# Shifting the ranks of a list scheduler's operations by a table, for two attention layers in one kernel

## The chip, the cores and the metric

The kernel runs on one core of a Trainium2 chip. The metric is device microseconds of one execution, as the median of several runs. The core has five engines that work side by side: PE (matmuls), DVE (VectorE), ACT (ScalarE), POOL (GpSimd) and SP (SyncE), which here issues every transfer. Each engine takes its instructions strictly in the order in which the program lists them, and engines wait for each other through semaphores. So the order written down for each engine is part of the program, and this change touches that order and nothing else.

## The reference: two attention layers, side by side

Both halves work on 2048 tokens of width 1024 with 32 heads of 32, and the result is their outputs next to each other.

```python
def _A_ref(x, wq, wk, wv, wo, beta):          # four segments of 512 tokens
    ...
    for s in range(N):
        qs, ks, vs = q[:, :, s], k[:, :, s], v[:, :, s]
        logits = jnp.einsum("bhqd,bhkd->bhqk", qs, ks) * scale + mask
        p = _softmax(logits, axis=-1)
        a_dot = jnp.einsum("bhqk,bhkd->bhqd", p, vs)
        pq = phi(qs)
        num = jnp.einsum("bhld,bhde->bhle", pq, M)
        den = jnp.einsum("bhld,bhd->bhl", pq, z)[..., None] + 1e-6
        outs.append(g * (num / den) + (1.0 - g) * a_dot)
        pk = phi(ks)
        M = M + jnp.einsum("bhld,bhle->bhde", pk, vs)
        z = z + jnp.einsum("bhld->bhd", pk)
    ...
    return o @ wo

def _B_ref(x, wqkv, w_phi, wo):               # linear attention
    ...
    pq = jnp.einsum("bhsd,hdf->bhsf", q, w_phi)
    pk = jnp.einsum("bhsd,hdf->bhsf", k, w_phi)
    phi_q = concatenate([_softmax(pq), _softmax(-pq)])
    phi_k = concatenate([_softmax(pk), _softmax(-pk)])
    kv = jnp.einsum("bhsf,bhsd->bhfd", phi_k, v)
    z  = jnp.einsum("bhsf->bhf", phi_k)
    o = einsum(phi_q, kv) / (einsum(phi_q, z)[..., None] + 1e-6)
    return o @ wo
```

## The kernel before

**Number formats.** Matmuls run in float16. An operand is scaled and split into a high and a low half, and a product is three matmuls (high by high, high by low, low by high: `product`, L370). The splits keep ACT (the high half), DVE or POOL (the low half) busy. The large projections of the second layer and the last projection of the first are Strassen products: seven instead of eight block products (`strassen`, L584 for its matmuls, and L1636 at the end).

**Stages.** First come 32 *units* of the first layer, one segment and four heads each (`produce`, `values`, `attend`). `produce` projects queries and keys (L370) and sends them by DMA into a stacked tile. `attend` forms scores twice: once to find row maxima (L846, with the masked maximum on DVE at L852), which go back as extra rows (L867, L872), and once for the exponentials (L947, ACT L951 and L953, DVE L954 for the low half, POOL L960 for the triangular mask). Then p times v (L983, summed by DVE at L987), the memory terms (L899 to L926) and the transposed result (L1015). Between them stand the folding of the weights of the second layer (`fold`, L1088, with the size at L1094), the splitting of its value weights (`weights_v`) and of its tokens, in pairs of tiles (`prepare`, L1134 and behind).

Then the pool of tiles is swapped for another, and eight pairs of token tiles go through keys and values of the second layer: a Strassen product (L584), the double softmax (`expo`: maxima and minima L1238, differences L1240 and L1242, exponentials L1245, sums L1248), the product with the inverse sums on POOL (L1354), a split (L1386, L1389) and the sums over tokens (L1396). Tile pairs 3, 4 and 5 are prepared only here, on the POOL lines L1153 and L1164. Next, the key sums are spread and split (L1419, L1440, L1443, L1445), and sixteen query tiles follow in the same way (L1550 to L1588), with an output projection each (`project`, L370 again). Eight Strassen products at L1636 end the kernel.

**What sets the order.** The code does not issue instructions where it describes them. It records each operation with its engine, a cost in microseconds, what it reads and writes, and a rank `prio` (`Graph.op`, L115). When all 16810 are recorded, `Graph.run` (L160) goes through them as a list scheduler: it keeps a clock for each engine, takes the engine that could start something first, and there, of the operations that could start by that time, the one with the lowest rank (ties go to the one that was recorded first). It counts latencies between engines, transfers on their queue, the port that DVE and POOL can't use at once, and the eight PSUM banks, which it hands out as it goes; for PE it prefers operations whose inputs are there with 0.4 us to spare. Only then is the instruction issued. In a unit u of the first layer the ranks are 2u for the projections, 2u + 0.9 for the values and 2u + 1 for attention; the keys of the second layer start at 100 and count 2 for a pair; the queries start at 118 and count 1 for a tile (a Strassen product has the rank of its tile less 1.2, a projection that of its tile and 1.1); the end has 135 and more.

Of the kernel before, what the change touches and what calls it, by code (L numbers as in the profile page):

```python
# [53 lines left out]
WPLAN = ((None, 0, 0), (None, 2, 1), (None, 3, 5), ((1, 0, "subtract"), 0, 3), ((3, 1, "subtract"), 1, 4),  # L54
         ((3, 0, "subtract"), 3, 2), ((2, 3, "subtract"), 2, 6))
EUP = 2.0 ** 15


def view(t, off, ap):
# [3 lines left out]
class Buf:  # L63
    def __init__(self, make, prev):
        self.make, self.prev, self.t = make, prev, None
        self.ops, self.writer, self.readers = [], {}, {}
        self.kind = None
# [11 lines left out]
class Graph:  # L79
# [10 lines left out]

    def __init__(self, pools):
        self.ops, self.tags, self.pools, self.opened, self.lines = [], {}, pools, {}, {}

    def buf(self, pool, shape, dtype, tag, bufs=1):
        q = self.tags.setdefault(tag, [])
        b = Buf(lambda: self.pools[pool].tile(shape, dtype, name=tag, tag=tag, bufs=bufs),
                (q[-bufs] if len(q) >= bufs else None, q[-1] if q else None, self.opened.get(pool)))
        q.append(b)
        return b
# [13 lines left out]
        return b  # L113

    def op(self, eng, dur, fn, r=(), w=(), prio=0, lat=0.0, short=False, port=False, need=(), kb=256):  # L115
        o = Op()
        o.short, o.port = short, port or eng == "POOL"
        o.eng, o.dur, o.fn, o.prio, o.lat, o.kb = eng, dur, fn, (prio, len(self.ops)), lat, kb
        o.banks = []
        ends, starts = set(), set()  # L120
        for b in need:
            if b.prev[0] is not None:
                ends.update(b.prev[0].ops)
        for write, accs in ((0, r), (1, w)):
            for acc in accs:
                b, key = acc if isinstance(acc, tuple) else (acc, None)
                old, last, opened = b.prev
                if old is not None:
                    ends.update(old.ops)
                if not b.ops and last is not None:  # L130
                    starts.add(last.ops[0])
                if opened is not None:
                    starts.add(opened)
                for k in (list(b.writer) if key is None else [key, None]):
                    if k in b.writer:
                        ends.add(b.writer[k])
                if write:
                    for k in (list(b.readers) if key is None else [key, None]):
                        ends.update(b.readers.pop(k, ()))
                    if key is None:  # L140
                        b.writer.clear()
                    b.writer[key] = o
                else:
                    b.readers.setdefault(key, []).append(o)
                b.ops.append(o)
                if b.kind is not None and b not in o.banks:
                    o.banks.append(b)
                    b.left += 1
        ends.discard(o)
        o.deps = [(d, 0) for d in ends] + [(d, 1) for d in starts - ends if d is not o]  # L150
        self.ops.append(o)
        return o
# [99 lines left out]
SP, PE, ACT, DVE, POOL = "SP", "PE", "ACT", "DVE", "POOL"  # L252
# [3 lines left out]
def tile_kernel(ctx: ExitStack, tc: tile.TileContext, ax, aw, awv, awo, beta, bx, bwqk, bwv, bphi, bwo, out):  # L256
# [70 lines left out]
    for t in vfb:  # L327
# [6 lines left out]
    gate1 = const.tile([128, H], F32, name="gate1")  # L334
    gates = G.fixed(gate)
    op(SP, 0.6, lambda: nc.sync.dma_start(gate, bass.AP(tensor=beta.tensor, offset=beta.offset, ap=[[0, 128], [1, H]])),
       w=[gates], prio=0.2, lat=2.0, kb=16)
    op(ACT, 0.2, lambda: nc.scalar.activation(gate, gate, AF.Exp, bias=0.0, scale=-1.0), w=[gates], prio=0.2)
    op(DVE, 0.2, lambda: nc.vector.tensor_scalar(gate, gate, 1.0, None, op0=OP.add), w=[gates], prio=0.2)
    op(DVE, 0.3, lambda: nc.vector.reciprocal(gate, gate), w=[gates], prio=0.2)  # L340
    op(DVE, 0.2, lambda: nc.vector.tensor_scalar(gate1, gate, -1.0, 1.0, op0=OP.mult, op1=OP.add), w=[gates], prio=0.2)
# [883 lines left out]
    def expo(ps, prio, sk, up=None):  # L1225
        port = ps not in psums

        def x3():
            return ps().rearrange("p (h d) -> p h d", d=32)

        def rep(v):
            return v[:, :, None].to_broadcast([128, 16, 32])

        mx = G.buf("b", [128, 2, 16], F32, "mx", 2)
        e = G.buf("b", [128, 16, 2, 32], F32, "e", 5)
        r = G.buf("b", [128, 16, 2], F32, "r", 5)
        for i, o in ((0, OP.max), (1, OP.min)):
            op(DVE, 0.6, lambda i=i, o=o: nc.vector.tensor_reduce(mx()[:, i, :], x3(), axis=AX.X, op=o),  # L1238
               r=[ps], w=[(mx, i)], prio=prio)
        op(DVE, 0.6, lambda: nc.vector.tensor_tensor(e()[:, :, 0, :], x3(), rep(mx()[:, 0, :]), op=OP.subtract),  # L1240
           r=[ps, (mx, 0)], w=[(e, 0)], prio=prio, port=port)
        op(DVE, 0.6, lambda: nc.vector.tensor_tensor(e()[:, :, 1, :], rep(mx()[:, 1, :]), x3(), op=OP.subtract),  # L1242
           r=[ps, (mx, 1)], w=[(e, 1)], prio=prio, port=port)
        for i in range(4):
            op(ACT, 0.41, lambda i=i: nc.scalar.activation(  # L1245
                e()[:, 4 * i:4 * i + 4], e()[:, 4 * i:4 * i + 4], AF.Exp, bias=0.0, scale=sk()[:, i:i + 1]),
               r=[e, sk], w=[(e, ("x", i))], prio=prio)
        op(DVE, 1.13, lambda: nc.vector.tensor_reduce(r(), e(), axis=AX.X, op=OP.add), r=[e], w=[r], prio=prio)  # L1248
        if up is not None:
            op(POOL, 0.15, lambda: nc.gpsimd.tensor_scalar(r(), r(), 1.0 / up, None, op0=OP.mult), r=[r], w=[r], prio=prio)  # L1250
        op(DVE, 0.27, lambda: nc.vector.reciprocal(r(), r()), r=[r], w=[r], prio=prio)
        return e, r

    def bc32(r):
        return r()[:, :, :, None].to_broadcast([128, 16, 2, 32])
# [86 lines left out]
    for at_, p in enumerate(SEQ):  # L1342
# [9 lines left out]
        def kout(i, hb, ps, es=es, sk=sk, P=P):  # L1352
            e, r = expo(ps, P, sk, EUP)
            op(POOL, 1.95, lambda: nc.gpsimd.tensor_tensor(e(), e(), bc32(r), op=OP.mult), r=[e, r], w=[e], prio=P)  # L1354
            es[i, hb] = e
# [60 lines left out]
    for q in range(4):  # L1416
        ps = bank("misc", [128, 512])
        for i in range(4):
# [3 lines left out]
        op(ACT, 0.5, lambda q=q, ps=ps: nc.scalar.activation(  # L1422
            zb()[:, 4 * q:4 * q + 4, :].rearrange("p a b -> p (a b)"), ps(), AF.Copy, scale=1.0 / EUP), r=[ps], w=[(zb, q)], prio=P)
    op(DVE, 0.1, lambda: nc.vector.tensor_reduce(big[:, 1:2], big[:, 1:6], axis=AX.X, op=OP.max),
# [283 lines left out]
```

## Time and profile before

| what | value |
|---|---|
| median of 3 runs | 1734.23 us (1733.72 to 1735.37) |
| the profiled execution | 1733.96 us |
| its span, first to last instruction | 1732.3 us |
| PE busy | 1697.2 us, 98% |
| DVE busy | 1384.0 us, 80% |
| ACT busy | 1157.8 us, 67% |
| POOL busy | 939.5 us, 54% |
| transfers | 273.62 MB |
| instructions | 39104 |

The span is what the trace shows from its first instruction to its last; the execution is 1.7 us longer. A row of a group names the line, the engine, the operation, the tile written and the tile read, their shapes, the number, then the busy time, the mean of one in ns, and the idle time ahead of them with what ended it. A row of the waits reads: who waited, for whom, microseconds in total, how often, the longest. A row of a stretch gives its start and end, its length, the busy time of PE, weight loads, DVE, ACT and POOL with the number of instructions, the granted share of PE's clock, the busy share of the DMA engines, and GB/s. A row of the timeline gives the start, the time taken, and then the operation.

### The profile page before, as it was taken

The page shows a single profiled execution, that of the slowest core. Times are in us where ns is not written, and L with a number is a line of the kernel's source. Part 1 is how long each engine was busy: PE and PEld are TensorE (multiplying, and loading weights), DVE is VectorE, ACT ScalarE, POOL GpSimd, SP SyncE. Part 2 cuts the span into 40 slices and gives each one's busy share as a digit, 9 for nine tenths or more (in the row PEclk, how much of TensorE's full clock was granted, in tenths as well). Part 3 has the DMA queues.
Part 4 walks back from the last instruction along what each step waited for, and adds up shares of the span by engine and source line. Part 5 has one row for each costly group of instructions (what it writes and reads, how often), then busy time and mean ns, then how long its engine had stood idle before and what let it go on. Part 6 is the DMA issues. An engine that isn't in the chain of part 4 may idle for free.

```text
span 1732.3 us, 39104 instructions
## 1 busy us (share of the span) xinstructions
PE 1697.2 (98%) x14664; PEld 1030.3 (59%) x14664; DVE 1384.0 (80%) x3269; ACT 1157.8 (67%) x2131; POOL 939.5 (54%) x1184
## 2 busy tenths in 40 slices
PE   8999999999999999999999999999999999999999
PEld 6667666767776676776754444444545555554444
DVE  6889899999997787889874988877978877786541
ACT  8788889888888798677772676765545544444331
POOL 3346477754478866656651777645737675440000
PEclk9999999999999999999999999999999999999999
DMA  6556455775666664743467474567413332234311
GB/s 210 160 166 185 151 169 174 223 209 169 224 181 185 188 165 122 227 162 106 136 179 262 131 240 130 180 211 251 161 44 118 103 111 85 63 139 146 122 66 63
DMA packets 194141, 273.62 MB, mean 158 GB/s; under 512 B 72224, under 2 KB 125216, under 8 KB 187424
## 3 DMA queue, kind: packets, MB, share of 16 engines
q1 hardware_dynamic: 193952, 271.13, 49.5%
q8 instruction: 115, 1.88, 0.4%
q14 instruction: 74, 0.61, 0.1%
HBM read 160.12 MB, written 85.00 MB: 142 GB/s over the span
## 4 chain that ended last, share of the span: by engine, by line
PE 40%; DVE 11%; ACT 2%; POOL 1%; issue 1%; POOLq 0%; ACTq 0%; DVEq 0%
PE proj L584 14%; PE misc L370 7%; PE proj L1636 5%; PE s L1636 2%; PE proj L370 2%; PE s L584 2%; DVE mx L1238 2%; PE misc L1636 1%; DVE r L1248 1%; PE pv L1582 1%; PE misc L584 1%; PE s L1569 1%; DVE e L1240 1%; DVE dn L1553 1%; DVE e L1242 1%; DVE pt L1389 1%
## 5 line engine op out<-in xcount | busy, mean ns | idle before, releaser
L370 PE MATMUL proj<-S,S 128*128 128x128 f16 (+1 forms) x3072 | 507.1, 300 | 4.3 <-DVE S L405 1.9
L370 PEld LDWEIGHTS <-S 128*128 128x128 f16 x4608 | 328.7, 98 | 151.2 <-issue 10.8
L584 PE MATMUL proj<-S,S 128*128 128x512 f16 x1584 | 360.6, 379 | 2.4 <-ACT cs L590 2.4
L584 PEld LDWEIGHTS <-S 128*128 128x128 f16 x2016 | 192.7, 98 | 221.7 <-issue 3.3
L960 POOL TENSOR_SCALAR_AFFINE_SELECT ph<-ph 128x256 f16<-128x256 f16 (+1 forms) x448 | 191.6, 450 | 172.5 <-DVE ph L954 133.7
L852 DVE CUSTOM_DVE_ANT_0 s<-s,causal 128x512 f32<-128x512 f32 (+3 forms) x512 | 242.6, 510 | 10.3 <-PE s L846 7.0
L954 DVE SCALAR_TENSOR_TENSOR ph<-s,ph 128x512 f16<-128x512 f32 x320 | 209.6, 683 | 51.5 <-ACT ph L953 49.3
L953 ACT ACTIVATE ph<-s 128x512 f16<-128x512 f32 x320 | 190.2, 659 | 0.3
L370 PE MATMUL misc<-S,ot 128*128 128x512 f16 x768 | 174.9, 380 | 0.0
L1245 ACT ACTIVATE e<-e,sk 128x256 f32<-128x256 f32 x256 | 113.4, 498 | 65.5 <-DVE e L1242 60.8
L370 PEld LDWEIGHTS <-ot 128*128 128x128 f16 x768 | 73.4, 98 | 81.8 <-issue 0.9
L846 PE MATMUL s<-S 96*128 96x512 f16 (+3 forms) x512 | 113.9, 299 | 2.2 <-DVE ph L954 1.6
L947 PE MATMUL s<-S 104*128 104x512 f16 (+3 forms) x512 | 113.1, 299 | 2.2 <-DVE ph L954 1.5
L951 ACT ACTIVATE s<-s,os 128x512 f32<-128x512 f32 x160 | 106.2, 717 | 6.9 <-PE s L947 5.3
L1550 POOL TENSOR_TENSOR e<-e,zb 128x512 f32<-128x512 f32 x64 | 80.2, 1277 | 55.7 <-DVE r L1248 35.1
L951 ACT ACTIVATE s<-s,bd 128x512 f32<-128x512 f32 x160 | 105.4, 705 | 6.5 <-PE s L947 6.4
L370 PE MATMUL proj<-wv,S 128*128 128x128 f16 x1536 | 101.8, 219 | 0.0
L983 PEld LDWEIGHTS <-ph 128*128 128x128 f16 x2560 | 87.3, 96 | 18.1 <-issue 2.2
L983 PE MATMUL pv<-vl,ph 128*128 128x66 f16 (+1 forms) x2560 | 91.9, 184 | 2.0 <-DVE oall L987 1.0
L1248 DVE TENSOR_REDUCE r<-e 128x32 f32<-128x1024 f32 x64 | 77.1, 1206 | 16.2 <-ACT e L1245 16.2
L1563 POOL TENSOR_TENSOR e<-e,r 128x1024 f32<-128x1024 f32 x32 | 61.9, 1938 | 34.5 <-DVE r L1561 27.5
L852 DVE DVE_READ_ACCUMULATOR2_ANT mt<- 128x1 f32 x512 | 72.6, 142 | 0.0
(344 smaller groups left out, 3344.1 us busy)
## 6 DMA issues: line engine op xcount, KB each, us to landing
S<-xf_d SPq DMA_DIRECT2D x126, 256.0 KB
S<-h SPq DMA_DIRECT2D x192, 128.0 KB
S<-wf_d SPq DMA_DIRECT2D x21, 1024.0 KB
st<-bwqk SPq DMA_DIRECT2D x64, 256.0 KB
out<-os SPq DMA_DIRECT2D x40, 256.0 KB
S<-aw SPq DMA_DIRECT2D x16, 512.0 KB
wa_d<-S SPq DMA_DIRECT2D x16, 512.0 KB
wf_d<-fo SPq DMA_DIRECT2D x32, 256.0 KB
```

Source lines behind the costliest of these rows:

```text
L370: op(PE, dur, lambda c=c, a=a, b=b, lv=lv, rv=rv: nc.tensor.matmul(pv(), lv(), rv(), start=(c == 0 and a + b == 0), stop=(c == n - 1 and a ...
L584: op(PE, 0.215, lambda n=n, a=a, b=b, lv=lv, rv=rv: nc.tensor.matmul(ps(), lv(), rv(), start=(start and n == 0 and a + b == 0), stop=(n == ...
L846: nc.tensor.matmul(ps()[:, o:o + 128 * i + 128], st()[0:96, 0, h, 128 * i:128 * i + 128], st()[0:96, 1, h, 0:128 * i + 128], start=True, s ...
L852: dve(0.12 + 0.00113 * n, lambda h=h, i=i, o=o, n=n: nc.vector.tensor_tensor_reduce(ps()[:, o:o + n], ps()[:, o:o + n], causal[:, 512 - n: ...
L947: nc.tensor.matmul(ps()[:, o:o + n], st()[0:104, 1, h, 128 * j:128 * j + 128], st()[0:104, 0, h, 128 * j:512], start=True, stop=True)
L951: act(0.59, lambda: nc.scalar.activation(ps(), ps(), AF.Exp, bias=0.0, scale=bdv()[:, 3, i2, 0:1]), r=[(bd, i2)], w=[ps])
L953: act(0.5, lambda: nc.scalar.activation(ph()[:, 0], ps(), AF.Copy, scale=2.0 ** 14), r=[ps], w=[(ph, 0)])
L954: dve(0.6, lambda: nc.vector.scalar_tensor_tensor(ph()[:, 1], ps(), 2.0 ** 14, ph()[:, 0], op0=OP.mult, op1=OP.subtract), r=[ps, (ph, 0)], ...
L960: nc.gpsimd.affine_select(pd, pd, pattern=[[0, n], [1, 128]], compare_op=OP.is_ge, fill=0.0, base=0, channel_multiplier=-1)
L983: nc.tensor.matmul(ps()[:, i, n0:n1], ph()[:, a, o:o + 128], vl()[:, j, h, n0:n1], start=(i == 0 and a == 0), stop=(j == min(i, 2)), skip_ ...
L1245: op(ACT, 0.41, lambda i=i: nc.scalar.activation(e()[:, 4 * i:4 * i + 4], e()[:, 4 * i:4 * i + 4], AF.Exp, bias=0.0, scale=sk()[:, i:i + 1 ...
L1636: op(PE, 0.215, lambda n=n, a=a, b=b: nc.tensor.matmul(ps(), v(a)[:, n, :], wform[w]()[:, b, n, :], start=(start and n == 0 and a + b == 0 ...
```

## The change

Consecutive operations that were recorded with the same rank form a *run*, on whichever engines they are; the runs are numbered from 0 in the order of recording, which gives 399. A new table `MOVES` holds, for each engine, offsets for some of these runs. `Graph.op` counts the runs and adds the offset of its engine and run to the rank. Operations that aren't in the table keep theirs, and the rule that picks operations, the costs, the operations themselves and what they depend on are untouched. The run is counted by the rank as it was handed in, so the offsets don't change the count.

```diff
+MOVES = {
+    "PE": {
+        20: -6.5, 22: -12.5, 76: -7, 79: -15.5, 83: -4, 96: -5, 101: 2, 102: 4, 104: 2, 107: 5.5, 108: 15.5, 113: 1.5,
+        128: -5.5, 134: 6.7, 139: -14.5, 140: 1.5, 145: 1.5, 149: 0.9, 156: 3.5, 160: 3.5, 162: 2.5, 164: 3.1, 167: 1.5,
+        168: 1.5, 171: 3, 179: -12, 183: 6.5, 186: 1.5, 192: 3, 196: 2, 199: -2, 200: 3.5, 201: 13.5, 203: -2.5, 206: -3,
+        207: -0.5, 208: -0.5, 212: -1.5, 213: -6, 215: 1, 217: -3.5, 223: -1.2, 224: -2.2, 247: 13.5, 270: -3.5, 272: 3, 281: 1,
+        284: -2, 297: -3, 299: 6.5, 302: 7.5, 309: -7, 312: -9, 313: 2.5, 317: -7, 327: -3, 331: 3.5, 337: -10.5, 363: 5.5},
+    "DVE": {
+        43: -2.5, 44: -0.5, 73: 2.5, 85: -10, 88: -5, 93: -6.5, 96: 1.5, 101: -5.5, 103: 7.5, 109: 1.5, 114: -6.5, 118: 2.5,
+        129: -3.5, 135: -2, 139: -13, 141: 4, 148: 8, 154: -1, 158: 7, 177: 4.5, 196: 0.5, 202: -1.5, 209: -0.9, 217: -2.5,
+        219: 10, 222: -1.5, 229: -3, 238: -43, 250: -15.5, 266: 1.5, 281: 0.5, 287: 1, 294: -1.5, 303: -2, 304: -1.5,
+        305: -18.5, 308: -15, 312: -14.5, 318: -3, 324: -0.2, 332: -6.5, 336: -3.5, 338: -7.5},
+    "ACT": {
+        45: -1.1, 68: 6.5, 79: -8.5, 85: -8, 93: -7.5, 98: 3, 120: 1.5, 121: -7.5, 135: 3, 141: 1.5, 142: -10, 143: -1.5,
+        147: 1.5, 148: -2.5, 149: -1.5, 153: 16, 155: 1, 177: -5, 179: 2, 180: 1, 187: -2, 198: 0.5, 206: -1, 209: 8, 212: 3,
+        214: 3.5, 216: -0.6, 218: 7, 219: 6.5, 224: 6, 232: -1, 238: -18, 257: -9, 270: -7, 326: -12.5, 328: -2.5, 333: -8.5},
+    "POOL": {
+        59: 0.5, 67: 5.5, 70: -0.5, 93: -6, 141: 5, 154: -8, 173: 3, 199: 12, 202: -3, 211: -16.5, 234: -5.5, 238: -29.5,
+        250: -2, 252: 1.5, 257: 0.5, 312: -11.5, 326: -7},
+    "SP": {
+        88: 5, 89: 2.5, 107: -2.5, 131: 3, 134: 21.5, 183: 8, 184: -7, 223: 6.5, 226: -9, 238: -37},
+}
...
     def __init__(self, pools):
         self.ops, self.tags, self.pools, self.opened, self.lines = [], {}, pools, {}, {}
+        self.job = (None, -1)
...
     def op(self, eng, dur, fn, r=(), w=(), prio=0, lat=0.0, short=False, port=False, need=(), kb=256):
+        if prio != self.job[0]:
+            self.job = prio, self.job[1] + 1
+        prio += MOVES.get(eng, {}).get(self.job[1], 0.0)
         o = Op()
```

Which operations stand behind the numbers can be counted off in the code. Runs up to 19 are the first loads, the first two units' projections and the first unit's attention; 20 and 22 are the scale and the bounds of the second value weights. Runs from there to 235 are the other units with the weights folded and the tokens split between them; of the entries for PE there, most shift a unit's projections (48 matmuls), its values (96) or one half of its attention. Run 238 is the preparation of tile pair 3, its loads, maxima, splits and stores, with the rank 100.5 before; 250 is that of pair 5; 247, 252, 257, 270, 272 and 281 are Strassen products and softmax of keys and values. Run 284 is the last pair's key sums, 287 the scaling and splitting of the key sums at L1432 to L1445. Runs 291 to 390 are the query tiles: 297, 309, 317, 331 and 337 are products of the Strassen steps, 299, 302, 313, 327 and 363 output projections, 312 and 326 the softmax denominators and transposes of a tile, and the entries for DVE there mostly the softmax of a block (maxima, differences, sums).

## The prediction

> **What bounds the kernel now.** I read the page first, for the engine that is never free, and then the view that cuts the span into stretches.
>
> ```profile
> span 1732.3 us, 39104 instructions
> ...
> PE 1697.2 (98%) x14664; PEld 1030.3 (59%) x14664; DVE 1384.0 (80%) x3269; ACT 1157.8 (67%) x2131; POOL 939.5 (54%) x1184
> ```
>
> ```profile
> core 0: us, PE busy (x) PEld busy (x) DVE busy (x) ACT busy (x) POOL busy (x), PEclk, DMA share, GB/s
> 0.00:100.00 100.00, 91.18 (x782) 64.99 (x783) 76.86 (x232) 77.57 (x134) 39.13 (x75) 0.95 0.60 187
> 100.00:200.00 100.00, 99.77 (x1122) 72.55 (x1121) 91.60 (x269) 86.92 (x157) 53.14 (x93) 1.00 0.54 163
> 200.00:250.00 50.00, 46.20 (x504) 31.52 (x502) 47.26 (x125) 48.74 (x90) 37.36 (x53) 1.00 0.57 189
> 250.00:500.00 250.00, 247.57 (x2725) 176.66 (x2723) 233.22 (x642) 209.04 (x377) 153.16 (x242) 1.00 0.64 194
> 500.00:900.00 400.00, 394.89 (x4254) 273.89 (x4254) 329.89 (x964) 317.29 (x571) 275.33 (x400) 1.00 0.57 167
> 900.00:1100.00 200.00, 197.46 (x1336) 98.22 (x1335) 155.51 (x267) 126.68 (x262) 121.81 (x122) 1.00 0.52 178
> 1100.00:1200.00 100.00, 99.86 (x712) 50.20 (x711) 76.54 (x126) 61.07 (x122) 51.48 (x47) 1.00 0.68 232
> 1200.00:1300.00 100.00, 93.14 (x658) 51.26 (x657) 87.88 (x171) 48.17 (x97) 55.87 (x44) 0.98 0.33 114
> 1300.00:1500.00 200.00, 199.57 (x1349) 102.95 (x1348) 161.96 (x280) 97.66 (x188) 126.38 (x96) 1.00 0.32 99
> 1500.00:1600.00 100.00, 99.35 (x647) 50.12 (x646) 75.54 (x135) 42.93 (x76) 25.83 (x17) 1.00 0.36 129
> 1600.00:1732.30 132.30, 128.18 (x594) 57.94 (x592) 47.77 (x70) 41.74 (x64) 0.00 (x0) 1.00 0.23 84
> ```
>
> PE is the bound: it stands still for 1732.3 - 1697.2 = 35.1 us in all. The change neither removes nor adds a matmul, so what it can win is idle time of PE. A stretch's length less its PE column gives, in order, 8.8, 0.2, 3.8, 2.4, 5.1, 2.5, 0.1, 6.9, 0.4, 0.7 and 4.1 us. The third view is that of PE's waits, longest first:
>
> ```profile
> PE pv L1582 <- DVE kls L1445: 4.0, 1, 4.0
> PE misc L381 <- ACT S L445: 3.2, 2, 1.7
> PE proj L584 <- ACT cs L590: 2.4, 3, 1.0
> PE misc L872 <- DVE mh L867: 1.9, 4, 0.9
> PE proj L370 <- DVE S L405: 1.9, 2, 1.4
> PE s L846 <- DVE ph L954: 1.6, 5, 0.5
> ```
>
> They are short and scattered, and nearly all end on DVE or ACT: PE's next planned matmul had an input a microsecond late. An order can mend such a wait only if some other ready matmul could have stood there. The longest wait has a second price, which stretches cut closer show, beside the two that do the same near 63 us:
>
> ```profile
> 1240.00:1256.00 16.00, 14.56 (x97) 7.99 (x96) 16.00 (x28) 7.32 (x15) 14.32 (x11) 1.00 0.12 34
> 1256.00:1262.00 6.00, 2.01 (x46) 1.68 (x46) 5.86 (x11) 3.27 (x8) 0.00 (x0) 0.97 0.16 45
> 1262.00:1264.00 2.00, 2.00 (x39) 1.83 (x36) 2.00 (x4) 0.83 (x2) 0.74 (x1) 0.50 0.00 0
> 1264.00:1266.00 2.00, 2.00 (x8) 0.76 (x9) 2.00 (x4) 0.60 (x1) 1.75 (x2) 0.74 0.00 0
> ...
> 62.00:64.00 2.00, 0.68 (x3) 0.28 (x3) 2.00 (x4) 2.00 (x5) 2.00 (x5) 0.89 0.46 135
> 64.00:67.00 3.00, 3.00 (x10) 1.26 (x9) 2.41 (x6) 3.00 (x6) 2.44 (x4) 0.51 0.28 87
> ```
>
> After the 4.0 us wait the granted clock falls to 0.50 for 1262 to 1264 and 0.74 for the two behind: 0.03 x 6 + 0.50 x 2 + 0.26 x 2 = 1.7 us of clock lost while PE counts as busy. Before it DVE is busy 16.00 of 16.00 us, so DVE holds this place. [...]
>
> **The change, part by part.** Nothing is removed or added among the instructions: 39104 before, and the same matmuls after; only the semaphore waits can differ by a few. 166 runs get a new rank: 59 on PE, 43 on DVE, 37 on ACT, 17 on POOL, 10 on SP. A rank decides only between operations that the planner has ready at the same time, so an offset delays or advances by what else was ready, never by its own number. All 166 entries name runs that have operations on that engine, so none is idle text.
>
> *Which part can't gain.* The lowest run in the table is 20, the scale matmul of the second value weights, which PE runs here:
>
> ```profile
> 102.64 0.28 PE L381 MATMUL misc<-wvb,one 128*128 128x1 f32 x2
> ```
>
> Both entries ahead of run 43 (20 and 22) only raise single matmuls that already ran next to their inputs, so the first 100 us with 8.8 us of idle time stay. The highest is run 363, the projection of the eleventh of sixteen query tiles, ahead of 1500 us; the 0.7 + 4.1 us behind that stay too. What is within reach is 0.2 + 3.8 + 2.4 + 5.1 + 2.5 + 0.1 + 6.9 + 0.4 = 21.4 us, plus the 1.7 us of clock: 23.1 us.
>
> *Attention, 200 to 250 us.* 3.8 us, but of the runs near it only seven have entries, none of them on PE. I take half: 1.9.
>
> *Attention, 250 to 900 us.* 2.4 + 5.1 = 7.5 us, and 112 entries, 41 of them on PE: projections of the next unit are put back or forward against the scores, mask, and p times v of the current one. That is the choice that fills a wait on DVE's ph, mh or twf. I take two thirds: 5.0.
>
> *Keys, 900 to 1200 us.* 2.5 + 0.1 us and 17 entries, with the largest ones: run 238, the splitting of tile pair 3, goes ahead by 43 places on DVE, 18 on ACT, 29.5 on POOL and 37 on SP, where its two loads and seven stores now stand ahead of the loads of the next pair. Two thirds: 1.7.
>
> *First queries, 1200 to 1300 us.* 6.9 + 1.7 us and 27 entries. Four groups of Strassen products of the first four query pairs gain 3 to 10.5 ranks on PE (one loses 3.5), and the first two output projections lose 6.5 and 7.5.
>
> ```profile
> 1263.93 11.07 PE L370 MATMUL misc<-S,ot 128*128 128x512 f16 x48
> ```
>
> So behind the 4.0 us wait PE spends 11.07 us on a projection that could stand later, while it had run out of Strassen products just before. But one wait of this stretch, on the last key sum, no order takes away, and DVE stays full:
>
> ```profile
> PE misc L1419 <- DVE za L1405: 1.3, 1, 1.3
> ```
>
> Two thirds: 5.7.
>
> The sum is 1.9 + 5.0 + 1.7 + 5.7 = 14.3 us.
>
> *What comes back.* A new order meets new late inputs. Its cost is not in the trace; the ends are 0 and what a dense stretch has now, 2.4 us in 250 (250 to 500), over the 1400 us that are reordered: 13.4 us. I take 3 us, near the low end, because the planner that weighs ready operations knows the costs well:
>
> ```profile
> L1248 DVE TENSOR_REDUCE r<-e 128x32 f32<-128x1024 f32 x64 | 77.1, 1206 | 16.2 <-ACT e L1245 16.2
> L1563 POOL TENSOR_TENSOR e<-e,r 128x1024 f32<-128x1024 f32 x32 | 61.9, 1938 | 34.5 <-DVE r L1561 27.5
> ```
>
> The code has 1.13 and 1.95 us for these, the trace 1.206 and 1.938. So 14.3 - 3 = 11.3 us go. The profiled execution took 1733.96 us (1.7 us outside its span); 1722.7 on that basis, and 0.3 more against the median of 1734.23: **1723.0 us**.
>
> **The rivals.**
>
> *More.* All 23.1 us within reach go and nothing comes back: 1734.2 - 23.1 = 1711. For it speaks that waits shorter than a matmul's modelled tail hide inside PE's busy time, so there is more than the view shows; against it, that DVE stays full around 1250 us.
>
> *Waits only move.* Each wait filled opens one of its size, or the ranks seldom change who is first: 1734. For it: no stretch between 250 and 900 us has more than 1.3 us of idle time in 100, so little is left that is easy.
>
> *Slower: run 238 jams POOL and DVE at the start of the keys.* The rows for 936 to 1000 us:
>
> ```profile
> L1354 POOL TENSOR_TENSOR e<-e,r 128x1024 f32<-128x1024 f32 x8 | 15.6, 1968 | 2.1 <-DVE r L1251 2.0
> L1164 POOL TENSOR_TENSOR kls<-zb,kls 128x512 f16<-128x512 f32 x7 | 8.0, 1155 | 1.2 <-ACT kls L1162 1.2
> L1153 POOL TENSOR_TENSOR zb<-zb 128x512 f32<-128x512 f32 x4 | 6.3, 1582 | 0.0
> L1242 DVE TENSOR_TENSOR e<-mx,cs 128x512 f32<-128x512 f32 x2 | 3.4, 1696 | 0.0
> L1242 DVE TENSOR_TENSOR e<-mx,proj 128x512 f32<-128x512 f32 x4 | 2.7, 674 | 0.0
> ...
> 950.00:965.00 15.00, 14.82 (x82) 7.05 (x81) 14.93 (x24) 6.83 (x15) 5.11 (x8) 1.00 0.26 88
> ```
>
> Run 238 is 8.0 + 6.3 = 14.3 us of POOL. Placed first, it pushes the products e by r, whose five buffers the next Strassen outputs need; then DVE can't empty PSUM, and PE stands still. Fully exposed that is +14.3 us, against the gains that the other stretches keep, 14.3 - 1.7 - 3 = 9.6 us: +4.7, so 1739. It decides once POOL reaches the first sums later than PE's other Strassen work lasts. For it: DVE is busy 14.93 of 15 us there, and beside POOL the same subtraction takes 1696 ns when both inputs are in SBUF against 674 with one in PSUM. Against it: POOL is busy only 5.11 of these 15 us, so most of the 14.3 finds room. [...]
>
> **How the numbers follow.** Forecast, 1717 to 1730: 0.58. More, 1711 to 1717: 0.17. Waits only move, within 0.2% of 1734.2 (1730.8 to 1737.7, about what a measurement of this kernel can tell from no change): 0.10. Slower by the jam, 1738 to 1744 (the upper end if the other stretches give only half their gain): 0.15. Faster is the first two, 0.75. The range runs from 1711, the lower end of the second, to 1734, the middle of the third: it leaves out 0.15 + 0.05 above. The high end of what may come back lies inside it: 1734.2 - 14.3 + 13.4 = 1733.3, and so does the low one, 1734.2 - 14.3 = 1719.9.
>
> **What would show it.** The count of instructions should stay at about 39104. PE's busy time should stay near 1697 less the 1.7 us of clock, with its idle time near 24 us instead of 35.1. Up to 100 us and from 1600 us the stretches should read as before, but shifted at the end. Between 1200 and 1300 us the wait of pv L1582 on kls should be under 1 us and the clock 1.00; if the wait stays at 4 us, 5.7 of my 14.3 us are wrong. Between 250 and 900 us the idle time should fall from 7.5 to about 2.5 us, and new waits should add up to some 3 us. I am wrong in sign if PE's idle time grows between 940 and 1060 us with POOL busy on L1164 and L1153 ahead of L1354. I am wrong in mechanism if the time falls by more than PE's idle time does.

## The result, and the profile after

The changed kernel takes 1721.86 us (median of 4 runs, 1721.07 to 1722.15) against 1733.97 us (median of 4); the ratio is 0.993, with a 95% interval of 0.9913 to 0.9947. Measured a second time, beside 17 runs of the kernel before, it took 1722.5 us against 1733.34, a ratio of 0.9943 (0.9928 to 0.9958). The forecast was 1723.0.

The page of the changed kernel, its span and its engines:

```profile
span 1720.4 us, 39087 instructions
## 1 busy us (share of the span) xinstructions
PE 1692.1 (98%) x14664; PEld 1030.8 (60%) x14664; DVE 1368.1 (80%) x3269; ACT 1159.6 (67%) x2131; POOL 939.8 (55%) x1184
```

The matmuls are the same 14664. PE stands still for 1720.4 - 1692.1 = 28.3 us instead of 35.1, and it is also *busy* 5.1 us less. So the span fell by 6.8 + 5.1 = 11.9 us, and two things have to be explained, not one. The stretches of the changed kernel, cut as before (start and end, length, then PE's busy time):

```profile
0.00:100.00 100.00, 90.34 (x791) 65.64 (x792) 77.11 (x238) 79.19 (x137) 38.55 (x76) 0.97 0.60 187
100.00:200.00 100.00, 99.84 (x1138) 73.06 (x1136) 93.70 (x270) 89.52 (x162) 54.82 (x93) 1.00 0.53 163
200.00:250.00 50.00, 49.53 (x557) 34.90 (x555) 47.73 (x133) 46.83 (x83) 40.04 (x55) 1.00 0.63 202
250.00:500.00 250.00, 247.40 (x2671) 174.40 (x2669) 228.15 (x635) 210.95 (x380) 151.52 (x241) 1.00 0.64 195
500.00:900.00 400.00, 398.48 (x4268) 276.66 (x4266) 321.31 (x953) 316.30 (x568) 274.65 (x395) 1.00 0.57 166
900.00:1100.00 200.00, 197.49 (x1339) 98.83 (x1338) 159.82 (x277) 128.61 (x269) 125.37 (x127) 1.00 0.57 187
1100.00:1200.00 100.00, 100.00 (x714) 50.29 (x713) 75.65 (x134) 62.76 (x127) 53.09 (x51) 1.00 0.67 227
1200.00:1300.00 100.00, 92.75 (x718) 51.62 (x718) 98.20 (x179) 53.87 (x106) 64.94 (x48) 1.00 0.37 124
```

**The idle time** went in two places: 3.8 to 0.5 us between 200 and 250, and 5.1 to 1.5 us between 500 and 900. Between 250 and 500 it stayed (2.4 and 2.6), and between 1200 and 1300 as well (6.9 and 7.2), where the forecast had its largest gain. The two longest of PE's waits there, in the changed kernel:

```profile
PE pv L1608 <- DVE pt L1599: 5.0, 3, 2.7
PE proj L610 <- ACT cs L616: 0.8, 1, 0.8
```

Lines are 26 higher than before (L1608 was L1582). The wait of 4.0 us for kls is gone, and the same group of matmuls now waits 5.0 us, in three waits, for the low half of a transpose, another product of the same engine: DVE is busy 98.20 of these 100 us, against 87.88 before. (The changed kernel is some 10 us further on in its work there, so the two rows don't hold quite the same operations.)

**The busy time** is in good part a matter of the granted clock. First five stretches of the kernel before, then four of the changed one:

```profile
12.00:16.00 4.00, 3.86 (x20) 3.86 (x21) 3.34 (x8) 4.00 (x8) 2.08 (x2) 0.57 1.00 410
19.00:23.00 4.00, 3.81 (x10) 1.35 (x10) 4.00 (x7) 4.00 (x7) 0.89 (x2) 0.57 0.42 133
...
1261.00:1265.00 4.00, 4.00 (x71) 3.19 (x68) 4.00 (x7) 1.79 (x3) 1.75 (x2) 0.58 0.00 0
...
60.10:63.50 3.40, 1.13 (x9) 0.62 (x8) 3.12 (x9) 3.40 (x9) 2.25 (x6) 1.00 0.19 48
63.50:67.00 3.50, 3.50 (x11) 1.45 (x10) 2.91 (x6) 3.50 (x7) 2.94 (x5) 0.51 0.32 105
```

```profile
11.00:18.20 7.20, 6.05 (x28) 6.06 (x29) 4.18 (x10) 5.62 (x10) 4.28 (x4) 0.53 1.06 359
19.00:23.00 4.00, 3.45 (x16) 1.51 (x16) 3.67 (x6) 4.00 (x8) 0.21 (x2) 1.00 0.36 113
...
59.00:62.50 3.50, 1.95 (x16) 1.52 (x16) 2.85 (x16) 3.50 (x8) 2.24 (x9) 1.00 0.01 1
62.50:66.00 3.50, 2.77 (x15) 1.44 (x15) 3.46 (x7) 3.50 (x8) 3.42 (x6) 1.00 0.57 152
```

In both traces the clock falls to 0.50 for 3.41 us at a time. The kernel before had it four times (near 12, 19, 63.5 and 1261.6 us), the changed one twice in a row, from 11.34 to 18.16 us. Where PE is busy throughout, one such drop adds 1.7 us to its busy time (the nine matmuls of L370 from 63.3 us take 3.79 us in the kernel before and 2.10 in the changed one, which has no drop there), so two drops fewer are up to 2 x 1.7 = 3.4 of the 5.1 us; for the other 1.7 no view has a row (PE's rows overlap, as at 101.78 us in the kernel before, where a matmul of 0.38 us stands 0.21 us ahead of the next, so my guess is that a wait that ends within such an overlap counts as busy). And of the 3.4 us only the 1.7 at 1261.6 lie where the table can act. Both kernels list the same operations in the same order, on every engine, up to 160 us. Within a trace the clock changes on a raster of 3.41 us: in the kernel before at 12.35, 15.77, 19.18, 22.59, 63.55, 66.97, 1261.63 and 1265.04 us (the 40.96 us between the fourth and the fifth are 12 steps, the 1194.66 between the sixth and the seventh 350), in the changed one at 11.34 and 18.17. So the two traces differ in where the steps of the raster (windows, counted back or on from a drop of the same trace) lie over the two waits near 61 us. Before, one window held both (1.13 of 3.40 us busy) and the clock was halved behind it; after, they fell into two (1.95 and 2.77 of 3.50) and it wasn't. That the place of the windows made the difference is my estimate. That the drop comes and goes from run to run is measured: e3 below lists the same operations there as the kernel before, whose trace has the drop at 63.5 us, and e3's granted clock is 1.000 over its whole span.

### The profile page after: what moved, and what is told of

Read it like the earlier page. It is cut to its first block, busy times and chain, and to the rows that moved or that the text cites. A ratio compares the mean times of both kernels' runs of the same rounds, so it can differ in the third digit from the quotient of the medians.

```text
span 1720.4 us, 39087 instructions
## 1 busy us (share of the span) xinstructions
PE 1692.1 (98%) x14664; PEld 1030.8 (60%) x14664; DVE 1368.1 (80%) x3269; ACT 1159.6 (67%) x2131; POOL 939.8 (55%) x1184
## 4 chain that ended last, share of the span: by engine, by line
PE 55%; DVE 9%; ACT 1%; issue 1%; DMA 0%; SPq 0%; ACTq 0%; DVEq 0%
PE proj L610 16%; PE misc L396 8%; PE proj L396 8%; PE proj L1662 5%; PE s L610 3%; PE s L1662 2%; PE misc L610 2%; PE s L973 1%; PE pv L1009 1%; PE misc L1662 1%; PE s L1595 1%; PE kv L1422 1%; PE pv L1608 1%; PE s L872 1%; DVE s L878 1%; DVE mx L1264 1%
## 5 line engine op out<-in xcount | busy, mean ns | idle before, releaser
L396 PE MATMUL proj<-S,S 128*128 128x128 f16 (+1 forms) x3072 | 501.8, 299 | 4.4 <-DVE S L431 1.6
L610 PE MATMUL proj<-S,S 128*128 128x512 f16 x1584 | 367.0, 379 | 1.7 <-ACT cs L616 1.2
L878 DVE CUSTOM_DVE_ANT_0 s<-s,causal 128x256 f32<-128x256 f32 (+3 forms) x512 | 242.9, 508 | 13.3 <-PE s L872 9.9
```

Source lines behind the costliest of these rows:

```text
L396: op(PE, dur, lambda c=c, a=a, b=b, lv=lv, rv=rv: nc.tensor.matmul(pv(), lv(), rv(), start=(c == 0 and a + b == 0), stop=(c == n - 1 and a ...
L610: op(PE, 0.215, lambda n=n, a=a, b=b, lv=lv, rv=rv: nc.tensor.matmul(ps(), lv(), rv(), start=(start and n == 0 and a + b == 0), stop=(n == ...
L878: dve(0.12 + 0.00113 * n, lambda h=h, i=i, o=o, n=n: nc.vector.tensor_tensor_reduce(ps()[:, o:o + n], ps()[:, o:o + n], causal[:, 512 - n: ...
```

## Experiments

The code's scheduler keeps a clock of its own, in its own costs, and returns where it ends (`Graph.run`): 1729.3 us for the kernel before and 1715.0 for the changed one. Two theories were tried with it. **L**: each group of entries fills waits near its own place, and the groups add up. **P**: an offset is worth something only in the list that it belongs to, and the scheduler's clock says what a list is worth. The edits cut the table; written as one line behind it they are

```diff
+MOVES = {e: {k: v for k, v in d.items() if k < 72} for e, d in MOVES.items()}          # e1
+MOVES = {e: {k: v for k, v in d.items() if 72 <= k < 236} for e, d in MOVES.items()}   # e2
+MOVES = {e: {k: v for k, v in d.items() if 236 <= k < 285} for e, d in MOVES.items()}  # e3
+MOVES = {e: {k: v for k, v in d.items() if 285 <= k} for e, d in MOVES.items()}        # e4
+MOVES = {e: {k: v for k, v in d.items() if k < 236} for e, d in MOVES.items()}         # e5
+MOVES = {e: d for e, d in MOVES.items() if e != "SP"}                                  # e6
+MOVES = {e: d for e, d in MOVES.items() if e == "POOL"}                                # e7
+MOVES = {e: {k + 1: v for k, v in d.items()} for e, d in MOVES.items()}                # e8
+del MOVES["POOL"][59]                                                                  # e9
+MOVES = {e: {k: v for k, v in d.items() if k == 238} for e, d in MOVES.items()}        # e11
```

| kernel | scheduler's clock | measured us | ratio to before, 95% interval |
|---|---|---|---|
| changed | 1715.0 | 1721.86, again 1722.50 | 0.993 (0.9913 to 0.9947), 0.9943 (0.9928 to 0.9958) |
| e1, runs to 71 | 1735.2 | 1747.15 | 1.0083 (1.0069 to 1.0097) |
| e2, runs 72 to 235 | 1746.0 | 1758.36 | 1.0155 (1.0136 to 1.0174) |
| e3, runs 236 to 284 | 1727.2 | 1726.89 | 0.9965 (0.9952 to 0.9977) |
| e4, runs from 285 | 1726.8 | 1730.14 | 0.998 (0.9971 to 0.9989) |
| e5, runs to 235 | 1717.7 | 1725.69 | 0.9961 (0.9949 to 0.9974) |
| e6, all but SP | 1745.1 | 1765.72 | 1.0188 (1.0173 to 1.0204) |
| e7, POOL alone | 1723.4 | 1728.60 | 0.9978 (0.9969 to 0.9987) |
| e8, on the next run | 1771.6 | 1779.65 | 1.0276 (1.0262 to 1.029) |
| e9, all but one entry | 1738.3 | 1756.04 | 1.0128 (1.0114 to 1.0142) |
| e11, run 238 alone | 1727.5 | 1732.24 | 0.9994 (0.9986 to 1.0003) |

**e1 and e2, the two halves of the attention units, each alone.**

> Only the nine entries for runs 0 to 71. Theory L (each group of entries fills waits near its own place, and the groups add up): what the two traces, laid over each other by the work that PE has done, show up to 330 us, less what is luck of the clock: -5 us against before, so 1729. Theory P (an offset is worth something only within the whole list that it belongs to, and the scheduler's own clock says what a list is worth; that clock ends at 1729.3 us for the kernel before, 1715.0 for the changed one and 1735.2 for this one): +6 us, about 1740. Nothing in between fits both.

> Only the 112 entries for runs 72 to 235, the rest of the attention units. Theory L: -4 us, so 1730. Theory P (the scheduler's clock ends at 1746.0, 16.7 above the kernel before): +14 to +17 us, 1748 to 1751.

Both were clearly slower than the kernel before, by 13 and 24 us. L falls: offsets that sit in a table which wins 12 us lose when they stand by themselves. P had the sign, and too small a size. Where time goes shows in e2, in three stretches and in the two largest of PE's waits from 380 to 460 us:

```profile
380.00:400.00 20.00, 17.58 (x98) 9.21 (x98) 17.59 (x55) 14.13 (x25) 11.76 (x19) 0.66 0.81 229
400.00:430.00 30.00, 27.41 (x215) 17.39 (x213) 23.54 (x71) 9.97 (x16) 3.59 (x3) 0.94 0.68 197
430.00:460.00 30.00, 23.80 (x278) 19.63 (x278) 24.76 (x63) 24.73 (x47) 12.87 (x27) 0.84 0.71 190
```

```profile
PE s L958 <- DVE ph L965: 3.1, 5, 1.1
PE s L857 <- DVE mt L863: 3.0, 5, 1.1
```

In the 80 us PE stands still for 2.4 + 2.6 + 6.2 = 11.2 us, in waits of 1.2 us at most, and loses up to 20 x 0.34 + 30 x 0.06 + 30 x 0.16 = 13.4 us of clock. The kernel before stands still for 1.4 us in the same 80 us, at full clock:

```profile
380.00:460.00 80.00, 78.64 (x854) 56.42 (x852) 76.70 (x211) 64.88 (x120) 38.26 (x72) 1.00 0.69 212
```

Both rows of waits are score products that wait for DVE; why this order brings them together, no view shows. No single wait is long; here a cluster of short ones was enough for the clock to fall, to 0.66, 0.94 and 0.84 in the three stretches.

**e3 and e4, the keys and the queries alone.**

> Only the 17 entries for runs 236 to 284, the keys. Theory L: -0.6 us, no difference. Theory P (the scheduler's clock ends at 1727.2): -2 us, so 1732. The jam of POOL and DVE by run 238, the rival of the prediction on the slow side: +5 us, since nothing else is there to pay for it.

> Only the 28 entries from run 285 on, the queries. The prediction gave these 5.7 us: 1728. Theory L by the two traces: -2.3 us, 1731.7. Theory P (the scheduler's clock ends at 1726.8): -2.4 us, 1731.6.

e3 was 6 us faster, more than either theory gave, and not slower, so nothing jams. Some of it is the clock: its six runs had 0.996 to 1.0, and 0.9978 on average, against 0.9949 for the 16 runs beside them. The trace says how much chance there can be. e3 lists the same operations in the same order as the kernel before, on every engine, up to 944 us of the scheduler's clock. Here are two rows of POOL in the kernel before, then the same two in e3, and e3's span:

```profile
157.80 1.00 POOL L960 TENSOR_SCALAR_AFFINE_SELECT ph<-ph 128x512 f16<-128x512 f16 x2
947.54 0.30 POOL L1250 TENSOR_SCALAR r<-r 128x32 f32<-128x32 f32 x1 [30.55 <-DVE r L1248]
```

```profile
154.50 1.00 POOL L971 TENSOR_SCALAR_AFFINE_SELECT ph<-ph 128x512 f16<-128x512 f16 x2
941.85 0.30 POOL L1261 TENSOR_SCALAR r<-r 128x32 f32<-128x32 f32 x1 [30.55 <-DVE r L1259]
core 0: 1723.5 us, clock 1.000
```

With none of the three early drops, e3 is 3.3 us ahead at the first row, and 5.7 us at the second, before any offset has had an effect. So of the 8.8 us between the two spans only 3.1 us come behind it, where the scheduler's clock has 2.1.

e4 gave 3.5 us, 0.2% (0.1 to 0.3), where the prediction had 5.7 for these runs.

**e5, the two losing groups together.**

> The 121 entries for runs 0 to 235 together, the two groups that alone were 13 and 24 us slower than before. Theory L (groups add up): +37 us, about 1771. Theory P (only the list as a whole counts; the scheduler's clock ends at 1717.7, 11.5 below the kernel before): 1719 to 1726.

1725.69: +13 and +24 make -7. This is the run that parts the theories most plainly.

**e6, all but the ten entries for SP, and e7, POOL's 17 entries alone.**

> All entries but the ten for SP. Theory L: SP only issues transfers, ten entries of 166, at most 3 us from the changed kernel, 1719 to 1725. Theory P (the scheduler's clock ends at 1745.1, 30 above the changed kernel): slower than before as well, 1745 to 1760, with PE standing still in many short waits and a lower granted clock behind them.

> The 17 entries for POOL alone. The rival, that an engine which is idle 46% of the span sets nothing: no difference. Theory P (the scheduler's clock ends at 1723.4, 5.9 below before): 1726 to 1730.

The ten offsets of transfers, 6% of the table, are worth 44 us to the rest of it; and POOL, idle for 45% of the span, makes the kernel 0.2% faster by its order alone. So an idle engine's order isn't free to choose. No view here follows how it acts; one way is that it decides which buffer, and so which operation, is ready next on the others. e6 was above P's range by 6 us; its granted clock was 0.986 to 0.99.

**e8, the same offsets on the wrong runs.**

> The same offsets, each put on the run behind the one that it names: a table as large, without its fit. The rival, that a shuffled order finds part of the gain because ranks by unit are too rigid: below 1734. Theory P (the scheduler's clock ends at 1771.6): +42 us and some loss of clock behind the new waits, 1780 to 1795.

46 us slower. That a more mixed order is good in itself is wrong.

**e9, one entry of 166 left out.**

> The changed kernel without one of its 166 entries: the smallest step in the table for POOL, +0.5 for run 59, four operations of 0.2 us. It keeps one addition of 1.25 us ahead of one product of 0.2 us at one place near 248 us, and nothing else is changed directly. Theory L: within 1 us of the changed kernel, 1721 to 1723. Theory P (the scheduler's clock ends at 1738.3, 23.3 above the changed kernel, since every later choice meets other ready times): 1740 to 1755, and the order the same as the changed kernel's up to about 248 us.

33.5 us slower than the changed kernel, from one entry of +0.5. The timeline of POOL, first in e9 and then in the changed kernel:

```profile
249.26 1.17 POOL L494 TENSOR_TENSOR fo<-quad,fo 128x512 f16<-128x512 f32 x1
250.38 0.21 POOL L729 TENSOR_TENSOR bd<-xsc,wgs 128x4 f32<-128x4 f32 x1
250.53 1.28 POOL L825 TENSOR_TENSOR pk<-pk,z 128x512 f32<-128x512 f32 x1
252.23 0.22 POOL L1015 TENSOR_TENSOR rd<-rd,sc 128x16 f32<-128x16 f32 x1 [0.42 <-DVE rd L1014]
```

```profile
248.06 1.16 POOL L509 TENSOR_TENSOR fo<-quad,fo 128x512 f16<-128x512 f32 x1
249.18 1.28 POOL L840 TENSOR_TENSOR pk<-pk,z 128x512 f32<-128x512 f32 x1
251.02 0.22 POOL L1030 TENSOR_TENSOR rd<-rd,sc 128x16 f32<-128x16 f32 x1 [0.57 <-DVE rd L1029]
251.20 0.20 POOL L744 TENSOR_TENSOR bd<-xsc,wgs 128x4 f32<-128x4 f32 x1
```

In e9 a bounds product of 0.21 us stands ahead of the addition of 1.28 us; in the changed kernel it stands two places behind. That is the first difference between the two programs on any engine, and the other engines' lists part within 17 us of it. From there each choice meets other ready times, and only 36% of PE's operations stand at the same place in the two lists. The 33 us are not lost here but later, all over:

```profile
250.00:500.00 250.00, 239.27 (x2574) 168.73 (x2573) 227.79 (x611) 205.26 (x369) 146.40 (x235) 0.99 0.60 184
500.00:900.00 400.00, 393.89 (x4195) 274.14 (x4192) 320.98 (x931) 306.60 (x546) 265.50 (x381) 1.00 0.57 165
900.00:1300.00 400.00, 385.40 (x2720) 198.75 (x2719) 331.94 (x589) 246.48 (x502) 235.04 (x232) 0.99 0.54 182
```

These are stretches of e9, and this is its page:

```profile
span 1755.0 us, 39078 instructions
## 1 busy us (share of the span) xinstructions
PE 1706.6 (97%) x14664; PEld 1035.5 (59%) x14664; DVE 1395.9 (80%) x3269; ACT 1160.5 (66%) x2131; POOL 939.0 (54%) x1184
```

The stretches have idle times of 10.7, 6.1 and 14.6 us, where the changed kernel has 2.6, 1.5 and 9.8. That is 17.6 us of its 34.6 us of span; PE's busy time grew by 14.5 us as well (1706.6 against 1692.1), of which its lower clock, 0.993 against 0.998, explains at most some 9.

**e10, the changed kernel again.**

> The changed kernel once more, for the luck of the clock's windows. Among 30 runs of the kernel before, each 0.001 of granted clock goes with 0.96 us, and the clock lay between 0.991 and 0.999. If the clock of 0.998 that the four runs of the changed kernel had is its own (its waits are too short to set the clock back), the median stays at 1721 to 1723 with a clock near 0.998. If it was luck, the median goes to 1723 to 1726 with a clock near 0.995.

1722.5 us, from 1721.24 to 1727.47, with clocks from 0.995 to 0.998: the median kept, the narrow spread of the first four runs was luck. Its trace shows the chance once more. Here, and in the changed kernel's first trace, PE waits 2.75 us for the same operation (L1608). In the first trace the clock stayed at 1.00 from 1236 to 1246 us; this time it fell behind the wait:

```profile
1236.00:1241.00 5.00, 2.25 (x22) 1.09 (x21) 5.00 (x9) 0.74 (x2) 4.46 (x4) 1.00 0.44 185
1241.00:1246.00 5.00, 4.93 (x49) 2.53 (x44) 5.00 (x11) 1.79 (x3) 0.00 (x0) 0.66 0.20 57
```

**e11, the jam alone.**

> The four entries for run 238 alone, the preparation of tile pair 3 put first on SP, DVE, ACT and POOL: the jam of the prediction's slow rival with nothing beside it. The rival: PE stands still while POOL works through 14.3 us of it, +5 to +14 us. Theory P (the scheduler's clock ends at 1727.5, 1.7 below before): 1730 to 1733, and POOL busy on it in the stretch from 950 us where it was idle.

No difference (0.9994, interval over 1). The stretch from 950 us in e11:

```profile
950.00:965.00 15.00, 15.00 (x84) 7.25 (x82) 12.65 (x25) 10.00 (x20) 9.24 (x9) 1.00 0.42 142
965.00:980.00 15.00, 15.00 (x71) 6.76 (x70) 11.78 (x19) 7.06 (x14) 14.46 (x14) 1.00 0.48 158
```

POOL takes the preparation up earlier (9.24 us busy instead of 5.11), DVE has less in this stretch (12.65 instead of 14.93), and PE stands still for nothing. The work found room, as the prediction's counter-argument had it.

## Why the prediction was right, and where it was not

The time was right within 1.1 us, and so were the bound (PE, with the same matmuls) and the refusal of the jam. The signs that the prediction named came out less well. It put PE's idle time near 24 us, and 28.3 were measured; between 250 and 900 us it put 2.5, and 4.1 were measured. Idle time fell by 6.8 us where those signs have 11.1, and PE's busy time by 5.1 where they have the 1.7 of the clock. (11.1 + 1.7 = 12.8 is also more than the 11.3 of its sum.) The wait on kls was gone, as it said, but not the time. One reading was off: its rival "waits only move" has at most 1.3 us of idle time in 100 between 250 and 900, which is the mean from 500 to 900; 300 to 400 has 1.8.

To see where the 11.9 us fell, the two traces can be laid over each other by work: for each matmul, the time that its kind needs in an undisturbed row is added up, and the times at which the two kernels have done the same amount are compared.

```text
work done, us   before at   after minus before
150             171         -1.6
250             279         -5.1
550             591         -2.5
850             905         -9.0
1150            1210        -9.6
1250            1322        -10.1
all             1732        -11.9
```

These are single traces, and chance moves such rows: against the kernel before, e3 is 5.7 us ahead at the place of the row for 850 with the same list of operations, and e4, whose list is also the same there, 0.75 us behind. So a difference of a few us in a row isn't shown to be the order's, and the terms below can be judged only roughly.

- *The first 100 us stay.* True of the order and wrong of the time: 1.6 us by 171 us, by the chance of the clock.
- *Attention, 200 to 250 us, 1.9.* It gave 3.5 between 171 and 279. There is no entry for PE here, and I took half for that reason; e7 shows that entries for POOL alone can win.
- *Attention, 250 to 900 us, 5.0 less most of the 3 that come back.* It gave 3.9 (-5.1 to -9.0), and the lines between show that it first gave 2.6 back.
- *Keys, 1.7.* 0.6.
- *First queries, 5.7.* 0.5. This is the step that failed: the wait moved to the next product of DVE, which was full, and the rival "waits only move" held in this stretch. The clock of 1.7 us, which is a part of the 5.7, was won there in one of two traces. Nor did the wait on kls need the entries for the queries: in e3, which has none of them, it is 0.3 us. By themselves these entries gave 3.5 us (e4).
- *Behind 1322 us, nothing.* 1.8, short waits by the sums.
- *Clock, 1.7, counted in the 5.7.* Up to 3.4 of PE's busy time in the trace, counted in the rows above, and half of it by chance. The time lost is less than that: a drop of 3.4 us at half speed is 0.001 of the span's mean clock, and over 30 runs of the kernel before each 0.001 goes with 0.96 us; e3's three drops fewer were 3.3 us ahead at 158 us, where 3 x 1.7 is 5.1. Over all runs, 47 of the kernel before averaged 0.995 and the ten of the changed kernel 0.997; at 0.96 us for each 0.001 that is about 2 us on average. The list that I gave for being wrong in mechanism has its last case fulfilled: the time fell by more than PE's idle time.

So the sum was right with terms that erred both ways, and by luck as much as by method. The premise below it was wrong in a deeper way. I priced the table by stages, as if each group of entries earned its part where it stands. e1, e2, e5, e6 and e9 show that groups have no price of their own: +13 and +24 make -7, and one entry of 166 holds 33 us. What kept the forecast low is that only 3 us, and not 13.4, were to come back, and for that it named the code's costs, which are close to the trace's. The scheduler's clock has 14.3 us for the change, and the chip gave 12.1 and 10.8; over eleven tables its difference to the kernel before has the chip's sign in ten, and in e11 the chip shows no difference. Its sizes hold less well: for e6 it has +16 us, and +33 were measured. Reading its end before and after would have given 1734.2 - 14.3 = 1719.9, no closer in number, but it prices the whole list and not its parts.

What stays open: e3's 6 us over six runs, of which the scheduler's clock has 2.1 and the slope of the clock some 2.8; why the wait on kls went in e3; and by what share the clock, rather than waits that the scheduler's model lacks, made e6 and e9 16 and 13 us slower against its end than the kernel before is.

## What to carry to other kernels

With a list scheduler that breaks ties by rank, a small change of rank is a new program from that point on: judge the whole list, and never the entry. A table of tuned ranks is good for the one recording that it was made for; a run more or less ahead of it (e8) costs four times what it won. Before two traces are laid over each other by stages, lay over each other two of one list: those of e3 and e4 are 6.4 us apart at 948 us with the same operations behind them. And on a kernel that PE bounds, count two prices for PE's waits, the idle time and the half clock behind a cluster of them (in e2 from 380 to 460 us 11.2 us of the one and up to 13.4 of the other).

## What the runs showed of the hardware

In the kernel before the clock fell to 0.50 for 3.41 us behind a window in which PE was busy for 1.13 of 3.40 us, with waits of 0.88 and 1.39 us and work between them; behind a window with 1.95 of 3.50 us in the changed kernel it stayed at 1.00. So that drop needed no wait as long as a window. PE's busy time alone doesn't decide it either. In e7 the clock fell behind a window with 2.56 us busy, and in the second trace of the changed kernel (e10) it did not behind one with 1.56:

```profile
56.40:59.81 3.41, 2.56 (x23) 2.39 (x23) 2.57 (x18) 3.41 (x8) 1.28 (x7) 1.00 0.07 12
59.81:66.63 6.82, 5.93 (x17) 2.51 (x17) 5.59 (x16) 6.50 (x13) 5.14 (x9) 0.50 0.24 78
```

```profile
60.66:64.07 3.41, 1.56 (x8) 0.73 (x8) 3.37 (x9) 3.41 (x9) 2.88 (x6) 1.00 0.33 82
64.07:67.50 3.43, 3.43 (x23) 2.20 (x22) 3.36 (x10) 3.43 (x7) 1.61 (x4) 1.00 0.25 74
```

The same two waits added 1.7 us to PE's busy time in the kernel before (3.79 us for the nine matmuls behind them) and nothing in the changed one (2.10). With one list of operations the drop begins at 63.5 us in the kernel before and at 59.8 in e7, and e3, with its clock of 1.000, has none.

In the kernel before DVE and POOL took turns at some of their operations. Here are two rows of a subtraction on DVE that reads two tiles in SBUF, the first with the row of POOL beside it, the second with POOL idle:

```profile
951.45 1.65 DVE L1242 TENSOR_TENSOR e<-mx,cs 128x512 f32<-128x512 f32 x1
951.03 1.52 POOL L1389 TENSOR_TENSOR pt<-e,pt 128x512 f16<-128x512 f32 x1 [0.74 <-ACT pt L1386]
...
1256.20 0.68 DVE L1242 TENSOR_TENSOR e<-mx,cs 128x512 f32<-128x512 f32 x1
```

The first ends at 953.10 us, 0.55 us behind POOL's, which ends at 952.55. So do the other seven rows of this group that start beside a product of POOL (1.64 to 1.75 us each); the seven with POOL idle take 0.68 us.

Of the kernel before, 30 runs had clocks from 0.991 to 0.999 and times from 1728.2 to 1737.9 us, 0.96 us for each 0.001. That spread of 9.7 us is as large as about half of the changes here, so a median of many runs, and the clock beside it, belong to each comparison.
